# Sliding-window attention into a gated MLP: two softmax groups transposed on TensorE, and one output store later in its queue

## The chip, the cores and the metric

The kernel runs on one core of a Trainium2 chip. The metric is the device time of one execution in microseconds. The engines of the core run side by side, each through its own list of instructions in order: TensorE (PE, with its weight loads as PEld), VectorE (DVE), ScalarE (ACT), GpSimd (POOL) and SyncE (SP), the last of which here only issues DMAs. An instruction waits until the semaphores that it names have the counts it needs, and everything behind it on its engine waits too. DMAs of POOL run in queue q0 of the profile, those of SP in q1.

## The reference

```python
# q, k, v: (8 batches, 8 heads, 576 positions, 64)
scores = q @ k.T / sqrt(64)
mask = (rel >= 0) & (rel < 64)          # rel = position of the query - position of the key
attn = softmax(where(mask, scores, -1e9))
x = (attn @ v) as (8 * 576 tokens, 512)
h = x @ w_in                            # (512, 2048)
out = (h * cos(h)) @ w_out              # (2048, 512), float32 out
```

Each query sees the 64 positions up to its own. Inputs and output are float32; the matmuls run in bfloat16.

## The kernel before

**Tiling.** Attention is cut into units: one batch, one pair of heads (four pairs) and one block of 64 queries (nine blocks in a batch). A unit needs 128 keys, so its scores are one tile of 128 (two heads x 64 queries) by 128 keys. Units are put together in groups of three or four, and every step of the softmax works on a group. The MLP runs over nine tiles of 512 tokens (`mt` 0 to 8), eight blocks of queries each, so a tile mixes units of two batches.

**A group's steps.** `g_scores_across` makes the scores on TensorE (tile `s_ps`, line 309). `g_max` adds the mask and takes the maximum on VectorE (L332). `g_exp` takes the exponential with its sums on ScalarE (tile `e`, L343). `g_inv` inverts the sums on VectorE (L350). `g_norm` multiplies on GpSimd into tile `w` (L357). `g_trans` then turns `w` so that keys lie on the partitions, in one of two ways. For a group in the set `direct`, TensorE transposes each unit into PSUM (tile `tw_ps`, L366), and `g_put` copies the result to tile `wT` on VectorE (L117, the line of a copy helper). For any other group, SP issues a DMA transpose from `w` to `wT` (L369). The tuple `DIRECT` lists the groups of `direct` behind batch 0's eight.

**Batch 2.** Its ten groups are numbers 12 to 21 in the count of `DIRECT`: four groups of one pair each with the query blocks 0 to 3 (12 to 15), two groups of two pairs with blocks 4 and 5 (16, 17) and four groups of one pair with blocks 6 to 8 (18 to 21). Before the change 12 to 15 are turned by DMA, 16 and 17 by TensorE, 18 to 21 by DMA.

**A tile of the MLP.** `values` multiplies `wT` with v into `o_ps` (L384), 16 matmuls for each pair of heads, 64 in all; `put_x` casts that to `xT` (L117). Then come 64 matmuls into `h_ps` (L451), the sine on ScalarE (L597), the product on VectorE into `gT` (L600), and 64 output matmuls into `out_ps` (L613): rows 0 to 255 of the tile first (`ms0` 0), then 256 to 511 (`ms0` 2). The results are copied to a tile `out_sb` (L117; one half on VectorE, the other on ScalarE), one `out_sb` for each `ms0`, and `store` writes it to memory by a DMA of SP (L471). `out_sb` has three buffers, taken in turn: that of tile 0's second half is the one of tile 2's first half.

**What sets the order.** The order of all instructions is written out. A list `plan` holds steps with a due time, in units of which a tile has 32 (16 in the `h_ps` stage, 16 in the output stage). `pump` emits all steps that are due, after every four output matmuls and after every four `h_ps` matmuls. Batch 2's groups are worked on in tile 1: the first four scores at 46.6, groups 12 to 15 at 46.6, 48.04, 49.48 and 50.92, and a group's later steps at fixed lags from that. A DMA transpose is due 3.8 after a group's time, a TensorE transpose 6.3 and its copy 6.6 after it (so 55.78 and 56.08 for group 14, 57.22 and 57.52 for group 15, if they are direct). The values of tile 2 are due at 62.99, at the end of tile 1. The two stores of tile 0 are due at 38 and 39, those of every later tile likewise 6 and 7 units into the second tile after it begins.

**Queues around it.** SP issues in order: the two stores of tile 0, the four DMA transposes of groups 12 to 15, then `turn` for batch 3 (`qX` in one DMA transpose, `kX` in two; L254), which wait for that batch's loads, then the DMA transposes of 18 to 21, then the two stores of tile 1. POOL works on `g_norm` and issues the loads of q, k and v (L169, L175) between.

Of the kernel before, what the change touches and what calls it, by code (L numbers as in the profile page):

```python
# [40 lines left out]
T = 2 * Q  # L41
LAGS = (0.2, 1, 3.2, 3.4, 3.8)
SKEW = 3
DIRECT = (0, 1, 2, 3, 4, 5, 8, 9, 16, 17, 26, 27)

# [17 lines left out]
def kernel(  # L65
# [47 lines left out]
    def bank(which, name):  # L113
        return ps.tile([128, 512], F32, tag=which, name=name)

    def copy(engine, out, in_):
        {"a": nc.scalar.copy, "p": nc.gpsimd.tensor_copy}.get(engine, nc.vector.tensor_copy)(out, in_)  # L117
# [165 lines left out]
    for b, cuts in enumerate(CUTS, 1):  # L283
        for cut in cuts:
# [5 lines left out]
            for of, lo, hi in cut:  # L290
                groups += [[(b, p, j) for p in range(p, p + of) for j in range(lo, hi)] for p in range(0, PAIRS, of)]
    direct = set(range(n_first)) | {n_first + i for i in DIRECT}

# [148 lines left out]
    def exp_table():  # L442
        nc.scalar.activation(small, small, AF.Exp, scale=0.0)
# [4 lines left out]
    def first(mt, ff, ks, start, stop):  # L448
        if start:
            st["h", ff] = bank(H_BANKS[ff], "h_ps")  # L450
        nc.tensor.matmul(out=st["h", ff], lhsT=w_in_sb[:, ks, ff * 128:ff * 128 + 128],  # L451
                         rhs=st["xT", mt][:, ks], start=start, stop=stop)

    def skewed(mt, ks, n):
        for ff in range(SKEW):
            first(mt, ff, ks, n == 0, n == PAIRS - 1)

    def last_rows(gT, o_sb):
        ms = MT // 128 - 1
        for which, lo, hi in (("O0", 0, LAST), ("S", LAST, d_model)):  # L460
            o_ps = bank(which, "out_ps")[:, lo:hi]
            for ff in range(n_ff):
                nc.tensor.matmul(out=o_ps, lhsT=gT[ff // 2][:, ff % 2, ms * 128:ms * 128 + 128],  # L463
                                 rhs=w_out_sb[:, ff, lo:hi], start=ff == 0, stop=ff == n_ff - 1)
            to = moe.tile([128, MT], F32, tag="sin", name="last_sb", bufs=4)[:, lo:hi] if lo else o_sb[:, 1, lo:hi]
            copy("d" if lo else "a", to, o_ps)
            (nc.sync if lo else nc.scalar).dma_start(out=out[n_mt * MT - 128:n_mt * MT, lo:hi], in_=to)

    def store(o_sb, mt, ms0, e, n):
        r0 = mt * MT + (ms0 + e) * 128  # L470
        nc.sync.dma_start(out=out[r0:r0 + n * 128].rearrange("(a p) f -> p a f", p=128), in_=o_sb[:, e:e + n])  # L471
# [3 lines left out]
    def at(time, fn, *args):  # L475
        plan.append((time, len(plan), fn, args))

    def pump(time):
        plan.sort(key=lambda x: x[:2])
        while plan and plan[0][0] <= time:  # L480
            _, _, fn, args = plan.pop(0)
            fn(*args)
# [93 lines left out]
    for mt in range(n_mt):  # L576
        base = mt * T
        gT = st["gT"] = [] if mt else st["gT"]
        if mt == 0:
            pump(base + n_ff - 1)  # L580
        if mt:
            for ks in range(PAIRS):
                pump(max([base - 1] + [time for time, _, fn, args in plan
                                       if fn is put_x and args[:2] == (mt, ks)
                                       or mt == 1 and fn is values and args == (mt, ks + 1)]))
                skewed(mt, ks, ks)
        for ff in range(n_ff) if mt else ():
            for ks in range(PAIRS):
                if ff >= SKEW:
                    first(mt, ff, ks, ks == 0, ks == PAIRS - 1)  # L590
            h_ps = st.pop(("h", ff))
            sin = moe.tile([128, MT], F32, tag="sin", name="sin", bufs=4)
            if ff % 2 == 0:
                gt = moe.tile([128, 2, MT], BF16, tag="gT", name="gT", bufs=n_ff // 2 + 2)
                gT.append(gt)
            e = ff % 2
            nc.scalar.activation(sin, h_ps, AF.Sin, bias=math.pi / 2.0)  # L597
            if ff == n_ff - 1 and mt < B - 1:
                exp_table()
            nc.vector.tensor_tensor(out=gt[:, e], in0=h_ps, in1=sin, op=ALU.mult)  # L600
            pump(base + ff)
        spans = ((0, 8), (8, 16)) if mt == 0 else ((0, n_ff),)
        for ms0 in range(0, MT // 128, 2):
            o_sb = moe.tile([128, 2, d_model], F32, tag="out", name="out_sb", bufs=3)
            o_ps = [bank(which, "out_ps") for which in (("O1",) if mt == n_mt - 1 and ms0 else ("O1", "O0"))]
            done = 0
            for lo, hi, e in [(lo, hi, e) for lo, hi in spans for e in range(2)]:
                ms = ms0 + e
                if mt == n_mt - 1 and ms == MT // 128 - 1:
                    last_rows(gT, o_sb)  # L610
                    break
                for ff in range(lo, hi):
                    nc.tensor.matmul(out=o_ps[e], lhsT=gT[ff // 2][:, ff % 2, ms * 128:ms * 128 + 128],  # L613
                                     rhs=w_out_sb[:, ff], start=ff == 0, stop=ff == n_ff - 1)
                    if ff % 4 == 3:
                        if ff == n_ff - 1:
                            copy("a" if e else "d", o_sb[:, e], o_ps[e])
                            if mt == n_mt - 1:
                                store(o_sb, mt, ms0, e, 1)
                        pump(base + Q + 4 * ms0 + done)  # L620
                        done += 1
            if mt < n_mt - 1:
                at(base + T + 6 + ms0 / 2, store, o_sb, mt, ms0, 0, 2)


# [28 lines left out]
```

## Time and profile before

| | us |
|---|---|
| median of three runs | 301.76 |
| lowest, highest of them | 301.65, 306.04 |
| the profiled execution | 302.51 |
| its span, first to last instruction | 300.7 |
| TensorE busy in it | 286.7 |
| ScalarE busy | 233.7 |
| VectorE busy | 221.2 |
| GpSimd busy | 171.5 |

The granted TensorE clock is full in the whole span (1.000). In the page, an engine's row gives its busy time; the chain that ended last is followed back from the last instruction, at each step to what released it. A row of a timeline has the start, the length, the engine, the line, the operation with its tiles and the number of instructions merged, and in brackets how long the engine idled before it and what released it. A row of DMA issues has the tiles, the queue, the count, the size of each and the median time from issue to landing.

```profile
PE   4899999999979999999999999999999999999996
DMA  8999999999999999999999999999994450011011
```

The first row is TensorE's busy share in tenths in 40 slices of the span, the second that of the DMA engines: both are nearly full for three quarters of the kernel.

### The profile page before, as it was taken

The page shows a single profiled execution, that of the slowest core. Times are in us where ns is not written, and L with a number is a line of the kernel's source. Part 1 is how long each engine was busy: PE and PEld are TensorE (multiplying, and loading weights), DVE is VectorE, ACT ScalarE, POOL GpSimd, SP SyncE. Part 2 cuts the span into 40 slices and gives each one's busy share as a digit, 9 for nine tenths or more (in the row PEclk, how much of TensorE's full clock was granted, in tenths as well). Part 3 has the DMA queues.
Part 4 walks back from the last instruction along what each step waited for, and adds up shares of the span by engine and source line. Part 5 has one row for each costly group of instructions (what it writes and reads, how often), then busy time and mean ns, then how long its engine had stood idle before and what let it go on. Part 6 is the DMA issues. An engine that isn't in the chain of part 4 may idle for free.

```text
span 300.7 us, 8012 instructions
## 1 busy us (share of the span) xinstructions
PE 286.7 (95%) x2703; PEld 145.7 (48%) x2738; DVE 221.2 (74%) x852; ACT 233.7 (78%) x781; POOL 171.5 (57%) x202
## 2 busy tenths in 40 slices
PE   4899999999979999999999999999999999999996
PEld 3578444444444445444544454445444444454443
DVE  4899898689757897789678967896789678136701
ACT  4997899779977799879987998799879986116600
POOL 8997357994998268945995599549704620000000
PEclk9999999999999999999999999999999999999999
DMA  8999999999999999999999999999994450011011
GB/s 167 184 198 211 207 162 119 142 153 136 229 130 156 138 233 181 141 157 231 122 158 158 234 154 160 165 231 152 151 173 154 92 162 30 2 70 73 0 70 70
DMA packets 165929, 44.01 MB, mean 146 GB/s; under 512 B 155008, under 2 KB 161152, under 8 KB 165888
## 3 DMA queue, kind: packets, MB, share of 16 engines
q0 software_dynamic: 99360, 18.06, 78.2%
q1 hardware_dynamic: 66384, 25.24, 47.3%
q8 instruction: 21, 0.34, 0.5%
q14 instruction: 20, 0.16, 0.2%
q10 hardware_dynamic: 144, 0.20, 0.2%
HBM read 36.70 MB, written 9.44 MB: 153 GB/s over the span
## 4 chain that ended last, share of the span: by engine, by line
PE 81%; DVE 5%; DMA 4%; POOL 3%; issue 3%; ACT 2%; SPq 0%; POOLq 0%; DVEq 0%
PE h_ps L451 36%; PE out_ps L613 33%; PE h_ps L423 5%; DMA wT<-w 3%; PE s_ps L309 3%; POOL w L357 2%; DVE s L332 2%; PE o_ps L384 2%; ACT e L343 1%; DVE xT L117 1%; PE out_ps L463 1%; DMA q_f<-in_q_dram 1%; PE tw_ps L366 1%; PE tq_ps L218 1%; PE tk_ps L218 1%
## 5 line engine op out<-in xcount | busy, mean ns | idle before, releaser
L613 PE MATMUL out_ps<-w_out,gT 128*128 128x512 bf16 x542 | 123.6, 379 | 1.8 <-issue 1.3
L451 PE MATMUL h_ps<-xT,w_in 128*128 128x512 bf16 x498 | 111.2, 379 | 0.9
L600 DVE TENSOR_TENSOR gT<-h_ps,sin 128x512 bf16<-128x512 f32 x128 | 84.9, 688 | 30.6 <-ACT sin L597 30.5
L357 POOL TENSOR_TENSOR w<-e,rden 128x512 bf16<-128x512 f32 (+1 forms) x75 | 73.0, 985 | 56.0 <-DVE rden L350 48.1
L343 ACT ACTIVATE e<-s,negm 128x128 f32<-128x128 f32 x256 | 98.6, 387 | 0.2 <-DVE negm L332 0.2
L597 ACT ACTIVATE sin<-h_ps 128x512 f32<-128x512 f32 x128 | 73.8, 599 | 29.7 <-PE h_ps L451 28.6
L613 PEld LDWEIGHTS <-gT 128*128 128x128 bf16 x560 | 52.8, 98 | 60.6
L451 PEld LDWEIGHTS <-w_in 128*128 128x128 bf16 x512 | 49.9, 98 | 59.1
L332 DVE CUSTOM_DVE_ANT_0 s<-s_ps,mask 128x128 f32<-128x128 f32 x256 | 57.9, 282 | 0.6 <-PE s_ps L309 0.3
L343 ACT ACTIVATION_READ_ACCUMULATOR e<-s,negm 128x1 f32 x256 | 47.8, 187 | 0.0
L175 POOL DMA_DIRECT2D v<-in_v_dram x40 | 34.1, 871 | 7.0 <-DMA w_out<-in_moe_w_out_dram 4.2
L117 ACT COPY out_sb<-out_ps 128x512 f32<-128x512 f32 (+1 forms) x18 | 10.2, 565 | 24.7 <-PE out_ps L613 19.0
L169 POOL DMA_DIRECT2D q<-in_q_dram x30 | 25.4, 881 | 4.4 <-DMA w_out<-in_moe_w_out_dram 3.0
L169 POOL DMA_DIRECT2D k<-in_k_dram x30 | 26.2, 876 | 2.7 <-DMA v<-in_v_dram 2.7
L117 DVE CAST xT<-o_ps 128x512 bf16<-128x512 f32 x28 | 18.3, 680 | 9.9 <-PE o_ps L384 9.7
L117 DVE COPY out_sb<-out_ps 128x512 f32<-128x512 f32 x18 | 12.3, 681 | 14.9 <-PE out_ps L613 14.5
L350 DVE RECIPROCAL rden<-den 128x4 f32<-128x4 f32 (+1 forms) x80 | 13.6, 171 | 11.1 <-ACT e L343 8.0
L332 DVE DVE_READ_ACCUMULATOR2_ANT negm<- 128x1 f32 x256 | 20.5, 80 | 0.0
L423 PE MATMUL h_ps<-xT,w_in 128*128 128x256 bf16 (+1 forms) x101 | 15.1, 295 | 0.3 <-issue 0.2
L384 PE MATMUL o_ps<-wT,v 128*64 128x64 bf16 x512 | 10.3, 197 | 1.9 <-DMA wT<-w 1.7
L384 PEld LDWEIGHTS <-v 128*64 128x64 bf16 x512 | 9.1, 112 | 5.9 <-issue 5.5
L117 DVE COPY v<-v 64x1024 bf16<-64x1024 bf16 (+1 forms) x19 | 11.5, 603 | 0.4
(59 smaller groups left out, 185.2 us busy)
## 6 DMA issues: line engine op xcount, KB each, us to landing
out_dram<-out_sb SPq DMA_DIRECT2D x16, 512.0 KB, 7.5
v<-in_v_dram POOLq DMA_DIRECT2D x32, 128.0 KB, 6.6
q<-in_q_dram POOLq DMA_DIRECT2D x24, 128.0 KB, 9.5
k<-in_k_dram POOLq DMA_DIRECT2D x24, 128.0 KB, 8.5
w_in<-in_moe_w_in_dram POOLq DMA_DIRECT2D x2, 768.0 KB, 12.1
w_out<-in_moe_w_out_dram POOLq DMA_DIRECT2D x1, 1024.0 KB, 13.3
w_out<-in_moe_w_out_dram POOLq DMA_DIRECT2D x2, 512.0 KB, 15.8
wT<-w SPq DMA_TRANSPOSE x60, 5.6
```

The costliest lines, as they stand in the source:

```text
L117: {"a": nc.scalar.copy, "p": nc.gpsimd.tensor_copy}.get(engine, nc.vector.tensor_copy)(out, in_)
L169: nc.gpsimd.dma_start(out=st[name, b][:n, c].rearrange("p (h d) -> p h d", h=H), in_=src.rearrange("h p d -> p h d"))
L175: nc.gpsimd.dma_start(out=vt.rearrange("p (h d) -> p h d", h=H), in_=v[b, :, c * 128:c * 128 + n, :].rearrange("h p d -> p h d"))
L332: nc.vector.tensor_tensor_reduce(out=s[:, u], in0=s_ps[:, u], in1=mask[:, 2 - j % 2 if j else 0], scale=-scale if b else -1.0, scalar=BIG, ...
L343: nc.scalar.activation(e[:, u], s[:, u], AF.Exp, bias=negm[:, u:u + 1], scale=1.0 if n < n_first else -1.0, accum_out=den[:, u:u + 1])
L357: (nc.gpsimd if engine == "p" else nc.vector).tensor_tensor(out=w[:, 0:u], in0=e[:, 0:u], op=ALU.mult, in1=rden[:, 0:u].unsqueeze(2).to_br ...
L384: nc.tensor.matmul(out=o_ps[64 * h:64 * h + 64, 64 * i:64 * i + 64], lhsT=vtiles[b % 2][:, max(j - 1, 0), 128 * p + 64 * h:128 * p + 64 * ...
L423: nc.tensor.matmul(out=st["h0", i].rearrange("p e t -> p (e t)") if i in WHOLE else st["h0", i][:, e], lhsT=w_in_sb[:, ks, ff * 128:ff * 1 ...
L451: nc.tensor.matmul(out=st["h", ff], lhsT=w_in_sb[:, ks, ff * 128:ff * 128 + 128], rhs=st["xT", mt][:, ks], start=start, stop=stop)
L597: nc.scalar.activation(sin, h_ps, AF.Sin, bias=math.pi / 2.0)
L600: nc.vector.tensor_tensor(out=gt[:, e], in0=h_ps, in1=sin, op=ALU.mult)
L613: nc.tensor.matmul(out=o_ps[e], lhsT=gT[ff // 2][:, ff % 2, ms * 128:ms * 128 + 128], rhs=w_out_sb[:, ff], start=ff == 0, stop=ff == n_ff - 1)
```

## The change

```diff
-DIRECT = (0, 1, 2, 3, 4, 5, 8, 9, 16, 17, 26, 27)
+DIRECT = (0, 1, 2, 3, 4, 5, 8, 9, 14, 15, 16, 17, 26, 27)
...
             if mt < n_mt - 1:
-                at(base + T + 6 + ms0 / 2, store, o_sb, mt, ms0, 0, 2)
+                at(base + T + (27.3 if mt == 0 and ms0 else 6 + ms0 / 2), store, o_sb, mt, ms0, 0, 2)
```

Groups 14 and 15, the third and fourth of batch 2, go from the DMA transposes of SP to TensorE: eight transposes of 128x128 stand between tile 1's output matmuls, four behind the 36th and four behind the 44th, and two copies from PSUM to `wT` are added on VectorE. The second store of tile 0 is due at 59.3 instead of 39. In SP's list that puts it behind the two transposes that are left of the four, behind batch 3's `qX` and `kX`, and behind the DMA transpose of group 18; those of 19 to 21 come after it. The lists of ScalarE and GpSimd stay the same.

## The prediction

> **What bounds the kernel now.** I read the page first, for the engine that fills the span, then the chain of waits for what sets the end, then the timelines around the one place where that chain leaves TensorE late in the kernel.
>
> ```profile
> span 300.7 us, 8012 instructions
> PE 286.7 (95%) x2703; PEld 145.7 (48%) x2738; DVE 221.2 (74%) x852; ACT 233.7 (78%) x781; POOL 171.5 (57%) x202
> ```
>
> TensorE is busy 95% of the span, so only what TensorE waits for or executes can move the end. From the chain that ended last, in order of time (start, length, what):
>
> ```profile
> 76.94 1.29 POOL w L357
> 78.24 1.20 SPq L369
> 79.53 8.78 DMA wT<-w
> 88.36 0.38 PE o_ps L384 x12
> ...
> 114.48 0.22 PE tw_ps L366 x4
> 114.71 1.73 PE out_ps L613 x8
> ```
>
> The softmax of batch 2's third group ends on POOL at 78.23, SP issues its transpose, then the one of the fourth group at 79.53, and that one lands at 79.53 + 8.78 = 88.31. Only then can TensorE finish the values of tile 2. TensorE's timeline there, and at the same place one tile later:
>
> ```profile
> 76.25 5.13 PE L613 MATMUL out_ps<-w_out,gT 128*128 128x512 bf16 x23 [0.16 <-issue]
> 81.50 0.40 PE L366 MATMUL tw_ps<-ident,w 128*128 128x128 bf16 x4
> ...
> 85.50 1.16 PE L384 MATMUL o_ps<-wT,v 128*64 128x64 bf16 x52
> 88.36 0.38 PE L384 MATMUL o_ps<-wT,v 128*64 128x64 bf16 x12 [1.70 <-DMA wT<-w]
> 88.67 3.63 PE L451 MATMUL h_ps<-xT,w_in 128*128 128x512 bf16 x15
> ...
> 118.31 1.20 PE L384 MATMUL o_ps<-wT,v 128*64 128x64 bf16 x64
> 119.54 2.75 PE L451 MATMUL h_ps<-xT,w_in 128*128 128x512 bf16 x11
> ```
>
> In tile 2 it takes 88.67 - 85.50 = 3.17 us from the first value matmul to the next stage, in tile 3 119.54 - 118.31 = 1.23 us. The difference, **1.94 us**, is the most that removing this wait can bring. The 52 matmuls that went before the wait are those of three pairs and of batch 1's units of the fourth; the 12 behind it need the fourth group alone. Over the whole kernel it is TensorE's only wait of this kind (total, times, longest):
>
> ```profile
> PE o_ps L384 <- DMA wT<-w: 1.7, 1, 1.7
> ```
>
> **Part 1: two groups move from DMA to TensorE.** Removed: two DMA transposes on SP with their landings. Added: eight 128x128 transposes on TensorE, two copies from PSUM on VectorE. A group's four transposes stand in the chain with 0.22 us, and the next matmul starts at 114.71, 0.23 after 114.48; the timeline's 0.40 counts the pipeline's tail, which overlaps. I take 0.24 a group, **0.48 us** in all. It lies wholly on the path, since TensorE has no gap there to hide it.
>
> The Trainium skill ("TensorE: Matmul & The Clock Gate", Part 4: PE-mode transpose) speaks against the change here: it gives about 275 ns for one 128x128 bf16 transpose inside a kernel and 390 ns alone. By it the eight would cost, as an estimate from that page, 2.2 to 3.1 us and eat the whole gain. The rows above contradict it for this kernel (four in 0.22 us between matmuls), so the sum goes by the rows.
>
> Does a new wait arise? The third and fourth groups' transposes fall due at 55.78 and 57.22 of the plan, which pumps them behind the 36th and the 44th of tile 1's 64 output matmuls. At 1.73/8 = 0.216 us each, the second two dozen starting at 76.25, that is 76.25 + 12 x 0.216 = 78.84 and, eight matmuls and one group of transposes later, 80.81. What they read comes from POOL:
>
> ```profile
> 76.94 1.28 POOL L357 TENSOR_TENSOR w<-e,rden 128x512 bf16<-128x512 f32 x1 [0.23 <-DVE rden L350]
> 78.45 1.04 POOL L357 TENSOR_TENSOR w<-e,rden 128x512 bf16<-128x512 f32 x1 [0.23 <-DVE rden L350]
> ```
>
> It is there at 78.22 and 79.49, so 0.6 and 1.3 us early. If that margin went, the output matmuls queued behind the transpose would stand still, microsecond for microsecond. Two more tiles go through the ring of three PSUM buffers that the score tiles use too; they take the buffers of the scores of the fifth and sixth groups, whose last read on VectorE begins here:
>
> ```profile
> 77.98 0.28 DVE L332 CUSTOM_DVE_ANT_0 s<-s_ps,mask 128x128 f32<-128x128 f32 x1
> 81.52 0.18 DVE L350 RECIPROCAL rden<-den 128x4 f32<-128x4 f32 x1 [1.16 <-POOL w L357]
> 83.59 0.42 DVE L117 COPY wT<-tw_ps 128x512 bf16<-128x512 bf16 x1
> 84.98 0.18 DVE L350 RECIPROCAL rden<-den 128x3 f32<-128x3 f32 x1 [0.58 <-ACT e L343]
> ```
>
> 78.26 is before 78.84, so no wait. The copies cost VectorE 0.42 us each. The first goes into the 1.16 us it idles before 81.52; the second pushes what follows by 0.42, which the idle 0.58 before 84.98 takes in. The value matmuls start at 85.50 + 0.48 = 85.98, when both have long ended. Cost of the copies: nothing. Without that idle time it would be up to 0.8 us on the casts.
>
> What is late next is the transpose of the second group. The four landed in 7.9 to 8.9 us (first row below: min, median, max), so it, issued behind the first of 75.05 and ahead of 78.24, was there by 78.24 + 8.9 = 87.1 at the worst; the second pair's values, its first readers, began near 85.8 with no wait, so it was in time then, and will be in time for values that start 0.48 later.
>
> **Part 2: the store.** Tile 0's second row blocks leave SP's queue at 71.8 and go behind the transpose of the seventh group (two more groups, the fifth and sixth, are TensorE's already). SP's own rows, and rows of landing times:
>
> ```profile
> DMA to landing us min/median/max: 7.9/8.6/8.9
> ...
> 71.29 1.04 SPq L471 DMA_DIRECT2D out_dram<-out_sb  x2
> 75.05 6.32 SPq L369 DMA_TRANSPOSE wT<-w  x4
> ...
> 95.80 6.97 SPq L369 DMA_TRANSPOSE wT<-w  x4
> ...
> 98.31 1.82 SPq L369 DMA_TRANSPOSE wT<-w  x1
> ```
>
> It takes the place now held by the issue at 98.31. The issue itself costs SP some 0.5 us and delays three transposes first needed at 118.31: nothing. The two in front of the second kX vanish, so the queue's first transposes come sooner, and the DMA engines carry one store less ahead of them. But the store has a reader: three buffers hold the output tiles, and the copy of tile 2's first output rows on VectorE overwrites the one that this store empties. So the change adds a wait there, with the score steps of batch 3 queued behind it on VectorE, and the exponentials on ScalarE waiting for those:
>
> ```profile
> 106.71 0.69 DVE L117 COPY out_sb<-out_ps 128x512 f32<-128x512 f32 x1 [0.40 <-PE out_ps L613]
> 107.32 0.28 DVE L332 CUSTOM_DVE_ANT_0 s<-s_ps,mask 128x128 f32<-128x128 f32 x1
> ...
> 108.17 0.39 ACT L343 ACTIVATE e<-s,negm 128x128 f32<-128x128 f32 x1
> ...
> DMA to landing us min/median/max: 7.5/8.3/9.2
> ```
>
> The last row is of the stores. With TensorE 1.46 us earlier, VectorE comes to that copy at 106.71 - 1.46 = 105.25. The row behind needs 107.32 + 0.28 = 107.60 for work that ScalarE starts at 108.17, so 0.57 us of waiting is free: the store costs nothing if it lands before 105.8 and gives the whole gain back if it lands after 105.8 + 1.46 = 107.3. Unmoved, SP would land it at 98.31 + 7.5 to 9.2 = 105.8 to 107.5. How much sooner SP is depends on the load that its second kX waits for:
>
> ```profile
> 83.91 0.73 POOL L169 DMA_DIRECT2D k<-in_k_dram  x1
> ...
> k<-in_k_dram POOLq DMA_DIRECT2D x1, 64.0 KB, 9.3
> ...
> 93.26 2.45 SPq L254 DMA_TRANSPOSE kX<-k  x1
> ...
> q1 hardware_dynamic: 160, 0.30, 88.8%
> q0 software_dynamic: 160, 0.02, 30.6%
> q0 software_dynamic: 413, 0.05, 80.0%
> ```
>
> That load lands at 83.91 + 9.3 = 93.2, and SP goes on at 93.26. The last three rows are packets, MB and share of a queue within one microsecond: SP's queue and the load queue from 78, with a store's rows in flight, and the load queue from 101, beside transposes. A store of 512 KB takes 0.52/0.30 = 1.7 us, in which the loads lose 1.7 x (413 - 160) = 430 packets, or 430/413 = 1.0 us. With one store less I estimate the landing 1.0 sooner, at 104.8 to 106.5, mostly in the free part, and take **0.2 us** of cost, between bounds of 0 and 1.46 (the whole gain).
>
> The Trainium skill ("DMA: Bandwidth & Descriptors", Anatomy of one DMA) has 2.0 us plus bytes over 436 GB/s for a DMA of the software path; by it a 512 KB store would land in an estimated 3.2 us, the wait could not exist, and the sum would be 0.2 us lower. The rows of 7.5 us and more say otherwise under this load, and they decide.
>
> **Sum.** -1.94 + 0.48 + 0.2 = -1.26 us, all on TensorE, and no later stage has a wait that would take it up: the chain from 119.54 on is matmuls. The profiled execution took 302.51 us with its span of 300.7; the median of the three runs is 301.76, 0.25% less, which changes a term of 1.3 us by nothing. Forecast: 301.76 - 1.26 = **300.5 us**.
>
> **Rivals.**
> - *The store holds VectorE* (slower). It lands late because the load queue or the transposes in front of it are no faster than now, or slower; a transpose of this queue that waits its turn has taken long:
>
> ```profile
> qX<-q SPq DMA_TRANSPOSE x1, 12.3
> ```
>
> At 98.31 + 12.3 = 110.6 the copy, the scores, the exponentials and through them the transposes of batch 3 on TensorE are 110.6 - 107.3 = 3.3 us later than before: 301.76 + 3.3 = 305.1. It decides against the change from a landing at 107.3 on. For it: every landing at this place is long. Against it: a store less before it. Chance 0.15, half of that between 301 and 302.4.
> - *Another wait takes the place of the removed one*: the second group's transpose, VectorE's copies or POOL's products are late by some tenths. Half the gain stays, 301.2. Against: margins of 0.6 us and more. 0.12.
> - *TensorE's transposes cost several times 0.06 us each* where the weights change between each: at the 0.40 us a group of the timeline 0.3 us more, 300.8; at 0.219 us for each by itself, the time that one is listed with, 8 x 0.219 = 1.75 and 301.8:
>
> ```profile
> L366 PE MATMUL tw_ps<-ident,w x74: 219/219/230, 12.4 to 116.4; 128*128 128x128 bf16 x74
> ```
>
>  Chance 0.05. The figures of the Trainium skill, "TensorE: Matmul & The Clock Gate", Part 4, would give an estimated 302.2 to 303.1.
> - *The store costs nothing and the lighter queue helps later*: no term of 0.2 and some tenths more, 299.9. 0.13.
>
> **How the numbers follow.** The forecast's own case (300.2 to 300.9) has 0.53; 0.02 is left for what I have not seen. The range 299.8 to 302.4 takes in the forecast, the two rivals between 300.8 and 301.8, most of the last one and the nearer half of the store's: 0.53 + 0.12 + 0.05 + 0.10 + 0.07 = 0.87. Two per cent (6.0 us), about what a measurement of this kernel can tell from no change, lies outside nearly all of it: faster by it has no mechanism (the whole wait is 1.94), 0.02; slower by it needs the store to land past 113, 0.04; within it 0.94.
>
> **What would show it.** Right: no wait of the values of tile 2 on a DMA, about 1.2 us from 85.98 to the next stage, two groups of transposes at 78.8 and 80.8 with no idle time before them, and every later row of TensorE some 1.3 us earlier. Wrong: VectorE's first output copy of tile 2 waiting for a DMA, with ScalarE idle behind it; or TensorE idle before its new transposes, on POOL.

## The result and the profile after

The changed kernel takes 301.57 us, the median of 21 runs (300.80 to 302.36), beside 302.40 us of the kernel before in as many runs (300.91 to 306.06). The ratio is 0.9959, with a 95% interval of 0.9939 to 0.9979: 1.2 us less, 0.6 to 1.8 by the interval. The two medians, which are of all runs, lie 0.83 us apart; the ratio leaves out executions more than 1.5% above the fastest of their kernel, in this comparison two, both of the kernel before. The forecast was 1.26 us less. By a margin of 2% that is the same time; the interval says that it is faster.

The first profile of the changed kernel would hide this: its span is 300.6 us, where that of before was 300.7. TensorE's timeline from the end of tile 1's `h_ps` stage to the start of tile 2's (start, length, engine, line, operation, count, idle before) shows both why the step worked and why this one execution gained nothing:

```profile
70.06 0.64 PE L309 MATMUL s_ps<-kX,qX 64*64 64x128 bf16 x32
70.63 5.35 PE L613 MATMUL out_ps<-w_out,gT 128*128 128x512 bf16 x24
75.91 0.58 PE L309 MATMUL s_ps<-kX,qX 64*64 64x128 bf16 x28
77.00 0.36 PE L309 MATMUL s_ps<-kX,qX 64*64 64x128 bf16 x12 [0.50 <-DVE negm L332]
...
87.19 1.20 PE L384 MATMUL o_ps<-wT,v 128*64 128x64 bf16 x64
88.41 3.83 PE L451 MATMUL h_ps<-xT,w_in 128*128 128x512 bf16 x17
```

The 64 value matmuls run in one piece, and the next stage begins 88.41 - 87.19 = 1.22 us after the first of them, as in tile 3 of the kernel before. The wait for the DMA transpose is gone. But the scores wait 0.50 us for VectorE, and VectorE's own timeline of that execution says what for:

```profile
69.93 0.69 DVE L600 TENSOR_TENSOR gT<-h_ps,sin 128x512 bf16<-128x512 f32 x1 [0.17 <-ACT sin L597]
71.64 0.68 DVE L117 COPY v<-v 64x1536 bf16<-64x1536 bf16 x1 [1.01 <-DMA v<-in_v_dram]
72.24 0.67 DVE L600 TENSOR_TENSOR gT<-h_ps,sin 128x512 bf16<-128x512 f32 x1
```

A copy within v, which stands at this place in both kernels, waited 1.01 us for the load of v, with a product and all maxima of tile 1 behind it. This load was issued before either edited instruction. The same copy had no such wait in the profile of before, nor in a second profile of the same changed kernel, whose span is 300.2:

```profile
70.62 0.64 PE L309 MATMUL s_ps<-kX,qX 64*64 64x128 bf16 x32
...
79.77 0.39 PE L366 MATMUL tw_ps<-ident,w 128*128 128x128 bf16 x4
79.99 1.89 PE L613 MATMUL out_ps<-w_out,gT 128*128 128x512 bf16 x8
81.72 0.39 PE L366 MATMUL tw_ps<-ident,w 128*128 128x128 bf16 x4
81.94 1.03 PE L613 MATMUL out_ps<-w_out,gT 128*128 128x512 bf16 x4
82.81 0.39 PE L366 MATMUL tw_ps<-ident,w 128*128 128x128 bf16 x4
...
86.80 1.20 PE L384 MATMUL o_ps<-wT,v 128*64 128x64 bf16 x64
88.03 5.34 PE L451 MATMUL h_ps<-xT,w_in 128*128 128x512 bf16 x23
```

So one span against another says little here, and I compare by **the stretch**: the time from the first scores of tile 1 to the first `h_ps` matmul of tile 2, which starts after whatever went before and ends after the edited part. It was 88.67 - 69.48 = 19.19 us before, and is 88.03 - 70.62 = 17.41 us here. (69.48 is the start of the same 32 score matmuls in the profile of before.) What comes behind the stretch doesn't differ: from the first `h_ps` matmul of tile 2 to the end of the span it takes 300.7 - 88.67 = 212.0 us before and 300.2 - 88.03 = 212.2 here, and 212.0 to 212.2 in all profiles below but the one of the late store. The new transposes, at 79.77 and 81.72, stand between output matmuls with no idle time before them.

### The profile page after: what moved, and what is told of

Read it like the earlier page. It is cut to its first block, busy times and chain, and to the rows that moved or that the text cites. A ratio compares the mean times of both kernels' runs of the same rounds, so it can differ in the third digit from the quotient of the medians.

```text
span 300.6 us, 8061 instructions
## 1 busy us (share of the span) xinstructions
PE 290.8 (97%) x2746; PEld 146.7 (49%) x2746; DVE 221.7 (74%) x854; ACT 234.0 (78%) x781; POOL 171.5 (57%) x202
## 4 chain that ended last, share of the span: by engine, by line
PE 76%; DMA 13%; POOL 4%; DVE 4%; issue 2%; SPq 0%; POOLq 0%; DVEq 0%
PE out_ps L613 35%; PE h_ps L451 32%; DMA v<-in_v_dram 8%; DMA k<-in_k_dram 4%; PE o_ps L384 3%; PE s_ps L309 3%; DMA v<-v 2%; POOL w L357 2%; PE out_ps L463 1%; DVE s L332 1%; POOL v L175 1%; PE tw_ps L366 1%; PE tk_ps L218 1%; PE s_ps L319 1%; DVE qT L240 0%
## 5 line engine op out<-in xcount | busy, mean ns | idle before, releaser
L613 PE MATMUL out_ps<-w_out,gT 128*128 128x512 bf16 x560 | 126.6, 379 | 0.0
L597 ACT ACTIVATE sin<-h_ps 128x512 f32<-128x512 f32 x128 | 73.8, 598 | 28.0 <-PE h_ps L451 26.9
L430 ACT ACTIVATE sin<-h_ps 128x512 f32<-128x512 f32 x16 | 9.1, 598 | 2.9 <-PE h_ps L423 2.8
L343 ACT ACTIVATE e<-s_ps,negm 128x128 f32<-128x128 f32 x32 | 11.2, 400 | 0.0
```

The lines of the kernel that those rows point to most:

```text
L343: nc.scalar.activation(e[:, u], s[:, u], AF.Exp, bias=negm[:, u:u + 1], scale=1.0 if n < n_first else -1.0, accum_out=den[:, u:u + 1])
```

## The experiments

Times are medians of all runs; each ratio is to runs of the kernel before on the same chip, with its 95% interval. The third column has the median of those runs of the kernel before. The stretch is read from one profile of each kernel.

| kernel | us | before, us | ratio | stretch, us |
|---|---|---|---|---|
| before | 302.40 | 302.40 | 1 | 19.19 |
| the change | 301.57 | 302.40 | 0.9959 (0.9939 to 0.9979) | 18.35 |
| the change, second profile | 301.45 | 303.60 | 0.9961 (0.9928 to 0.9994) | 17.41 |
| transposes moved only | 301.53 | 302.96 | 0.9938 (0.9909 to 0.9967) | 17.46 |
| store moved only | 301.98 | 302.96 | 0.9969 (0.9933 to 1.0005) | 17.37 |
| store moved, one group moved | 301.61 | 302.96 | 0.9958 (0.9929 to 0.9987) | 17.25 |
| the change, transposes doubled | 302.29 | 302.96 | 0.9959 (0.9922 to 0.9995) | 17.85 |
| the change, store later still | 301.90 | 303.60 | 0.9982 (0.9945 to 1.0020) | 17.41 |
| the change, copy of v later | 301.50 | 303.60 | 0.9931 (0.9900 to 0.9962) | 17.40 |
| store moved only, copy of v later | 301.94 | 303.60 | 0.9966 (0.9934 to 0.9998) | 17.24 |
| one group, copy of v later | 301.41 | 302.41 | 0.9966 (0.9939 to 0.9993) | 17.24 |

The intervals are 0.4 to 0.75% wide and overlap nearly everywhere, so the times say that the wait is worth removing and no more. What tells the kernels apart is the stretch.

**The transposes without the store.**

```diff
 (kernel before)
-DIRECT = (0, 1, 2, 3, 4, 5, 8, 9, 16, 17, 26, 27)
+DIRECT = (0, 1, 2, 3, 4, 5, 8, 9, 14, 15, 16, 17, 26, 27)
```

> Groups 14 and 15 on TensorE, the store of tile 0 left where it was. Theory (the gain is the vanished wait of tile 2's values, less 0.24 us for each group moved): the last DMA transpose is the second group's and is there in time even with the store ahead of it, so no wait of the values on a DMA and -1.46 us, ratio near 0.995, the same as the whole change. Rival (the store ahead of the transposes was what made them late, and the move to TensorE pays for nothing): the second group's transpose still lands late behind the two stores, a wait of several tenths stays, ratio 0.998 to 1.001.

Ratio 0.9938, no wait of tile 2's values on a DMA, the stretch 17.46 us, as with the whole change (17.41). The two transposes that are left landed as slowly as before behind the two stores (min, median, max of the two):

```profile
DMA to landing us min/median/max: 7.5/7.7/7.8
```

They were in time all the same. The theory holds: moving two groups is enough by itself.

**The store without the transposes.**

```diff
 (kernel before)
-                at(base + T + 6 + ms0 / 2, store, o_sb, mt, ms0, 0, 2)
+                at(base + T + (27.3 if mt == 0 and ms0 else 6 + ms0 / 2), store, o_sb, mt, ms0, 0, 2)
```

> The store moved, groups 14 and 15 left with the DMA transposes. Theory A (the four transposes are late because 512 KB of the store, some 1.7 us, run ahead of them in the same queue): the fourth lands 1.7 us sooner, the wait shrinks from 1.94 to about 0.2 us and nothing is paid on TensorE: -1.7 us, ratio 0.994, better than the whole change. Theory B (their lateness is the time from the issue on SP to the landing, whatever runs ahead): the wait stays at 1.5 to 1.9 us, ratio 0.998 to 1.001.

The wait is gone here too. All four DMA transposes are there, and this is how long they took to land:

```profile
DMA to landing us min/median/max: 5.3/5.9/6.4
```

Against 7.9, 8.6 and 8.9 before, that is 2.5 to 2.7 us less, where 1.7 had been estimated from the store's bytes. So B, by which it makes no difference what runs ahead, falls, and A holds: the transposes were late because of the store. Whether the store holds them up as the one ahead in SP's queue, or as a load on the 16 DMA engines on which the page counts the packets of both queues, no run here tells apart. The time alone would not show the gain: the ratio, 0.9969, has an interval that reaches 1.0005. Some 0.3 us of that time lie outside the span, why is open: a run takes 2.09 us more than its span here (median), 1.79 in the kernel before. The stretch is 17.37 us, not the 0.48 us shorter than the whole change that A also implies; the next two say why.

**One group instead of two.**

```diff
 (changed kernel)
-DIRECT = (0, 1, 2, 3, 4, 5, 8, 9, 14, 15, 16, 17, 26, 27)
+DIRECT = (0, 1, 2, 3, 4, 5, 8, 9, 15, 16, 17, 26, 27)
```

> The store moved, group 15 alone on TensorE, group 14 by DMA. Theory: the third group's transpose, issued at 78.2 of the run before, was there for the values already, so the wait is gone with half of the price: -1.94 + 0.24 = -1.7 us, ratio 0.994. Rival (both groups are needed): a wait of several tenths on the third group's transpose, ratio 0.996 or more.

The stretch is 17.25 us. TensorE's timeline has the 64 value matmuls of tile 2 in one piece:

```profile
76.07 0.75 PE L309 MATMUL s_ps<-kX,qX 64*64 64x128 bf16 x40
...
81.08 0.39 PE L366 MATMUL tw_ps<-ident,w 128*128 128x128 bf16 x4
81.30 1.03 PE L613 MATMUL out_ps<-w_out,gT 128*128 128x512 bf16 x4
82.23 0.40 PE L366 MATMUL tw_ps<-ident,w 128*128 128x128 bf16 x4
...
86.23 1.20 PE L384 MATMUL o_ps<-wT,v 128*64 128x64 bf16 x64
```

The third group's DMA transpose was in time, and the price of one group is not visible. The timed ratio, 0.9958 (0.9929 to 0.9987), holds the theory's 0.994 as well as the rival's 0.996, so this too rests on the profile. A wait of values on a DMA transpose does stand in this execution, 0.60 us at 56.60, but that is tile 1's, ahead of the stretch and of both edits.

**Every new transpose twice.**

```diff
 (changed kernel, g_trans)
-            for i in range(u):
+            for i in [i for i in range(u) for _ in range(2 if n - n_first in (14, 15) else 1)]:
                 nc.tensor.transpose(t_ps[:, i], w[:, i], ident)
```

> The whole change, with each of the eight transposes of groups 14 and 15 done twice into the same place. Theory: 0.24 us more for each group, +0.48 us against the whole change, so a ratio near 0.9975 where the whole change has 0.996; in the timeline eight transposes stand in 0.48 us. Rival (the price that a transpose shows when it is listed alone, 0.219 us, or more): +1.75 us or more, ratio 1.002 or more.

TensorE's timeline of this kernel:

```profile
76.79 0.75 PE L309 MATMUL s_ps<-kX,qX 64*64 64x128 bf16 x40
...
80.08 0.61 PE L366 MATMUL tw_ps<-ident,w 128*128 128x128 bf16 x8
80.52 1.89 PE L613 MATMUL out_ps<-w_out,gT 128*128 128x512 bf16 x8
82.25 0.61 PE L366 MATMUL tw_ps<-ident,w 128*128 128x128 bf16 x8
82.70 1.03 PE L613 MATMUL out_ps<-w_out,gT 128*128 128x512 bf16 x4
83.56 0.39 PE L366 MATMUL tw_ps<-ident,w 128*128 128x128 bf16 x4
```

Eight transposes take 0.44 us to the next matmul (80.52 - 80.08), where four take 0.22 in the change (79.99 - 79.77): 55 ns each. The stretch is 0.44 us longer than the change's 17.41. The price of 0.24 us a group is right, and the rival of 0.219 us a piece is wrong by a factor of four. The timed ratio, 0.9959, is that of the change; its interval reaches from 0.9922 to 0.9995 and can't tell 0.44 us. The profile alone shows this price.

Why is a further group dear and the first one free? From the second scores of tile 1 to the fifth group's transposes, the same work but for the added groups, it takes 81.50 - 75.33 = 6.17 us before (75.33 is the second scores' start there), 82.23 - 76.07 = 6.16 with one group, 82.81 - 76.48 = 6.33 with two (76.48 likewise, second profile of the change), 83.56 - 76.79 = 6.77 with two done twice. TensorE's weight loads show the cover. Of the kernel before:

```profile
81.50 0.23 PEld L366 LDWEIGHTS <-w 128*128 128x128 bf16 x4 [0.62 <-POOL w L357]
```

And of the change:

```profile
82.64 0.37 PEld L366 LDWEIGHTS <-w 128*128 128x128 bf16 x4 [0.17 <-POOL w L357]
```

The fifth group's transposes, TensorE's already, waited for GpSimd's product. The new transposes stand ahead of that wait and fill it: of 0.48 us only 6.33 - 6.17 = 0.16 us lengthens the path against this profile of before. In two more profiles of before (the last experiment below) the wait for GpSimd is longer and stands in TensorE's own rows:

```profile
82.50 0.40 PE L366 MATMUL tw_ps<-ident,w 128*128 128x128 bf16 x4 [0.42 <-POOL w L357]
```

```profile
82.91 0.40 PE L366 MATMUL tw_ps<-ident,w 128*128 128x128 bf16 x4 [0.34 <-POOL w L357]
```

There the same piece takes 82.50 - 76.05 = 6.45 and 82.91 - 76.53 = 6.38 us without any new transpose (76.05 and 76.53 are the second scores' starts). The mean of the three is 6.33, as long as the piece of the change: how much of the 0.48 us is paid depends on how long GpSimd would have been waited for in that execution, and here it is between nothing and 0.16.

**The store later still.**

```diff
 (changed kernel)
-                at(base + T + (27.3 if mt == 0 and ms0 else 6 + ms0 / 2), store, o_sb, mt, ms0, 0, 2)
+                at(base + T + (33 if mt == 0 and ms0 else 6 + ms0 / 2), store, o_sb, mt, ms0, 0, 2)
```

> The whole change, but the moved store goes behind all four remaining transposes of batch 2, next to the two stores of tile 1. Theory (the store has a reader, VectorE's first output copy of tile 2, which takes up to 0.57 us of lateness without a cost and passes on the rest): issued at about 101.5 it lands 7.5 to 9.2 us later, at 109 to 110.7, VectorE waits 3 us or more there, and TensorE behind it; 109 to 110.7 less 107.3 is 1.7 to 3.4 us slower than the kernel before, ratio 1.006 to 1.011. Rival (the copy's wait does not reach TensorE, which has other buffers to write to and scores made ahead): VectorE waits as long, but the ratio stays near 0.996.

The new wait that the change could have made is here in full. VectorE's, ScalarE's and TensorE's rows of the timeline (the idle time in brackets):

```profile
109.00 0.69 DVE L117 COPY out_sb<-out_ps 128x512 f32<-128x512 f32 x1 [2.09 <-DMA out_dram<-out_sb]
110.00 0.40 ACT L343 ACTIVATE e<-s,negm 128x128 f32<-128x128 f32 x1 [1.19 <-DVE negm L332]
110.38 0.42 PE L309 MATMUL s_ps<-kX,qX 64*64 64x128 bf16 x16 [0.98 <-DVE negm L332]
...
119.91 1.20 PE L384 MATMUL o_ps<-wT,v 128*64 128x64 bf16 x64
```

VectorE waits 2.09 us for the store, ScalarE 1.19 for VectorE's maxima, TensorE 0.98 for its scores' buffers. From tile 2's first scores, at 103.01 in this execution, to tile 3's values it takes 119.91 - 103.01 = 16.90 us; in the second profile of the change, 117.66 - 101.93 = 15.73. So 1.17 of the 2.09 us reach TensorE: 0.92 are slack, where 0.57 had been reckoned. The mechanism is right and the rival, that it does not reach TensorE, falls. VectorE's wait is shorter than the 3 us that were expected because this execution came to the place later, after a 1.9 us wait of tile 1's first scores on their keys: the store had less to be late by. The expected time, 1.006 to 1.011, was wrong: timed, this is the worst version of the change, 0.9982 (0.9945 to 1.0020), not shown to differ from the kernel before in either direction. That interval holds the rival's 0.996 too, so it is the profile that decides against it. The median is 0.45 us above that of the change in the next experiment, less than the 1.17 of this profile; why it loses less is open.

**The whole change once more.**

> The whole change once more, beside the others of this call: ratio 0.996 as measured, with a profile in which the values of tile 2 wait for no DMA. If the wait of VectorE's copy of v on its load, 1.01 us in the changed kernel's first profile, is chance, it is not there or shorter, and the span is 299 to 300; if it belongs to the change, it is there again.

The ratio came out the same, 0.9961, the span 300.2, a little above the 299 to 300 expected, and the copy of v did not wait. Of the ten profiles here with the copy at this place, three of them of the kernel before, only the first of the change has that wait, so the wait belongs to that one execution and not to the change. In this profile the chain of waits that ended last is matmuls and transposes alone in the stretch, with no piece of idle time above 0.16 us.

**The copy of v out of the way.**

```diff
 (changed kernel; the same edit in the kernel with the store moved only)
-            for time, part in ((13.5, 0), (19.9, 2), (21.7, 3)):
+            for time, part in ((24.6 if b == 2 else 13.5, 0), (19.9, 2), (21.7, 3)):
```

> The whole change, with VectorE's first copy within v of batch 2 moved from the end of tile 1's h stage, where it can wait for the load of v and hold the products and the maxima behind it, to an idle place of VectorE behind the fifth group of maxima. Theory (that wait costs TensorE up to 1.2 us in some executions): the median falls by 0.2 to 0.8 us against the whole change, ratio 0.993 to 0.995, and the highest times fall. Rival (the wait has slack in most executions, or the copy is in the way at its new place): the same ratio, 0.996, or more.

> The store moved and that copy moved, the transposes of groups 14 and 15 left to DMA. If the store was the cause of their lateness, this is the whole change less 0.48 us of TensorE: ratio 0.992 to 0.994, the fastest of all. If the DMA transposes are late again in part of the executions: 0.995 or more, with a wait of the values on a DMA.

With the change: ratio 0.9931, inside the range of the theory, but its median, 301.50, is that of the change beside it (301.45), where 0.2 to 0.8 us less was expected, so this is not shown to be a gain. The highest of 12 times is 302.12, no sign of a shorter tail: the highest of the first 21 of the change was 302.36. With the store moved only: 0.9966, no wait, not the fastest, so the hope of 0.992 to 0.994 was wrong. The stretches, 17.40 and 17.24 us, differ by 0.16 us; those of the same pair with the copy in its old place, 17.41 and 17.37, by 0.04, since there the store-only kernel waited 0.24 us for GpSimd at the fifth group.

**One group, and the copy of v later.** Both edits above together.

> The store moved, group 15 alone on TensorE, and VectorE's first copy within v of batch 2 at its later place. Theory (one group's transposes are hidden in TensorE's wait for GpSimd's product of the fifth group; the later copy takes a DMA wait off VectorE): from tile 1's first scores to tile 2's first h matmul about 17.25 us, as with one group before, and a ratio of 0.993 to 0.995. Rival (what is left of the differences is spread between executions): a ratio of 0.996 to 0.998, as the others have.

The stretch is 17.24 us as expected, the ratio 0.9966: the rival was right about the time.

**The kernel before, two more profiles.**

> The kernel before, once more with a profile. Theory (the wait of tile 2's values is as long as the DMA queue of that execution makes it): a wait of another length than 1.7 us, between 0 and some 5 us, and a span that differs from 300.7 by about the difference, besides what other DMA waits of the execution add. Rival (the wait is 1.7 us in every execution and the spread of the times comes from elsewhere): 1.5 to 1.9 us again.

> As the look before it: another length of the wait by the theory, 1.5 to 1.9 us by the rival.

TensorE's timeline of the first, then of the second:

```profile
70.19 0.64 PE L309 MATMUL s_ps<-kX,qX 64*64 64x128 bf16 x32
...
86.51 1.01 PE L384 MATMUL o_ps<-wT,v 128*64 128x64 bf16 x52
89.14 0.38 PE L384 MATMUL o_ps<-wT,v 128*64 128x64 bf16 x12 [1.62 <-DMA wT<-w]
89.45 3.84 PE L451 MATMUL h_ps<-xT,w_in 128*128 128x512 bf16 x16
```

```profile
70.67 0.64 PE L309 MATMUL s_ps<-kX,qX 64*64 64x128 bf16 x32
...
86.91 1.07 PE L384 MATMUL o_ps<-wT,v 128*64 128x64 bf16 x52
89.32 0.38 PE L384 MATMUL o_ps<-wT,v 128*64 128x64 bf16 x12 [1.34 <-DMA wT<-w]
89.63 3.63 PE L451 MATMUL h_ps<-xT,w_in 128*128 128x512 bf16 x15
```

The wait is there each time, 1.70, 1.62 and 1.34 us, and the stretch 19.19, 19.26 and 18.96. In these three it varies little, as the rival had it (the last lies a little under its 1.5). The mean stretch is 19.14 us, and the change saves 19.14 - 17.41 = 1.73 us of it. The values account for all of that: from the first value matmul to the next stage it takes 3.17, 89.45 - 86.51 = 2.94 and 89.63 - 86.91 = 2.72 us, which is 1.94, 1.71 and 1.49 over the 1.23 of tile 3, 1.71 in the mean.

Three profiles don't settle the question for all executions. The fastest runs of the kernel before are as fast as those of the change: beside the first four versions of the table one took 300.88 us with a span of 299.1, where the lowest of the change is 300.80 with 299.0. With the 212.0 us behind the stretch and at least the 69.48 ahead of it that every profile shows, 299.1 leaves at most 17.6 us for the stretch, so that execution can hardly have had the wait, unless it was faster ahead of the stretch than any profile here. If the wait is absent in part of the executions, the timed gain must be smaller than 1.73 us, as it is; no profile here shows such an execution, nor one of the slowest, which take up to 306 us.

## Why the prediction was right

- **What bounds it.** Right: TensorE's one long wait on a DMA transpose is gone, and the next stage follows 1.22 us after the first value matmul, where 1.23 was forecast. Its 1.94 us are those of one execution; the mean of three profiles is 1.71. (In the two later ones TensorE also waits 0.2 and 0.3 us for a DMA transpose in tile 1.)
- **The price of the transposes.** Right for each (55 ns in a row, 0.22 to 0.24 us a group), wrong for the sum. The step that said that 0.48 us "lies wholly on the path, since TensorE has no gap there to hide it" failed: TensorE had a gap behind them, at the fifth group's transposes, which waited for GpSimd. 0.16 us was paid against the first profile of before, and nothing against the mean of its three.
- **No new wait on GpSimd, on PSUM buffers or on the copies.** Right: no idle time stands before the new transposes in the profiles of the change, and none of the three late things came.
- **The store.** The wait that it could add on VectorE is real (late store), but at the place where the change puts it, it cost nothing. In the first profile it was issued at 96.56 and landed 8.0 us later, at 104.56, while VectorE came to the copy at 106.44. SP got there 1.75 us sooner than the 98.31 of before; 1.0 had been taken. The 0.2 us of cost was not there.
- **What moving the store is for.** This was missed. The prediction counted it only as a cost and a help to the loads, and gave the vanished wait to TensorE's transposes alone. The store moved alone removes the wait as well: the transposes were late because its 512 KB ran ahead of them. The two edits each do the whole work, and together they do it once.
- **The sum.** -1.94 + 0.48 + 0.2 = -1.26 was forecast; the times give -1.2 with an interval of 0.6 to 1.8, the stretch -1.73. Against the first profile of before the terms are -1.94 + 0.16 + 0 = -1.78, against the mean of three -1.71 and nothing else. So two costs were put in that the runs don't show, and that the sum meets the timed gain to within 0.1 us is in part luck. The forecast time, 300.5, is 1.07 us under the measured 301.57; 0.64 of it is the base, since the kernel before took 301.76 us in the three runs known then and 302.40 in 21.
- **Open.** The stretch is shorter in every profile of an edited kernel than in the three of before, but times of one kernel spread over 1.3 to 5.8 us, and the first scores of tile 1 start anywhere from 69.48 to 71.70 us in the thirteen profiles, in which TensorE has the same work up to there. What decides that in each execution was not settled; one late copy of v and one late key transpose were seen, each in one execution.

## What to carry to other kernels

When a DMA is waited for, look first at what runs ahead of it in its own queue: moving a bulk store behind the small urgent transfers took the wait away in the profile without spending anything on the busiest engine. When work is added to that engine, look for its waits behind the place as well as before it: work put ahead of a wait for another engine was free here up to the length of that wait. And when one profile differs from another by less than the spread of the times, compare a stretch that starts just ahead of the edit and ends just behind it, not the spans.

## What the runs showed of the hardware

The 128x512 DMA transposes of batch 2 landed 7.5 to 8.9 us after their issue in the four profiles with two 512 KB stores ahead of them in SP's queue, and 4.8 to 7.3 us after it in the nine with one. Where all four were DMA transposes, the median was 8.1 to 8.6 us behind two stores and 5.5 to 5.9 behind one; where two were left, 7.7 behind two stores (one profile) and 6.2 to 6.9 behind one. So one store more cost them between 0.8 and 3.1 us, beside the 1.7 us that its bytes take at the rate seen.
